# Filler matmuls ahead of the first back, transposes in the fronts' PSUM banks, other ranks in the planner: a retention layer with a mixer

## The chip, the cores and the metric

The kernel runs on one core of one Trainium2 chip. The metric is the device time of one launch in microseconds (us), from the first to the last instruction and what lies around them. The engines are PE (matmuls), DVE and ACT and POOL (elementwise work), and SP, which here issues DMAs. Each works through its own queue in the order of the program; they meet at semaphores.

## What is computed

A recurrent retention layer over 768 positions with 8 heads, and behind it an MLP mixer over positions and channels:

```python
B, H, S, D = q.shape                      # 4, 8, 768, 64
gamma = 1.0 - 2.0 ** (-5.0 - np.arange(H, dtype=np.float32))
scale = 1.0 / np.sqrt(D)
for t in range(S):
    state = gamma[None, :, None, None] * state + np.einsum('bhd,bhe->bhde', k[:, :, t], v[:, :, t])
    y[:, :, t] = scale * np.einsum('bhd,bhde->bhe', q[:, :, t], state)
x = np.ascontiguousarray(y.transpose(0, 2, 1, 3)).reshape(B, S, H * D)
# mixer: w_tok1 768x256, w_tok2 256x768, w_ch1 512x1536, w_ch2 1536x512
xt = x.transpose(0, 2, 1)
h = np.maximum(xt @ w_tok1, 0.0) @ w_tok2
u = x + h.transpose(0, 2, 1)
h2 = np.maximum(u @ w_ch1, 0.0) @ w_ch2
return (u + h2).astype(np.float32)
```

## The kernel before

The recurrence is cut into six chunks of 128 positions. A *front* works on one batch b in four pairs p of heads, a *back* does the channel mixing of one batch. A pair goes through these steps, with the lines of the kernel before: three loads of k, q and v (SP, L209 and L213); a cast of k with the heads' decay on DVE (L230) and casts of q and v on POOL (L237); six transposes each of k and q on PE (L250) into a PSUM tile of the tag tp, and a copy from it to SBUF, on ACT for q, on DVE (first batch) or ACT for k (L259); ten small matmuls for the chunks' states (L272), which DVE chains in U (L281, L284) and ACT and DVE round to r (L291, L295); the scores in two halves of six matmuls (L311), masked by DVE (L318); the output y in two halves (L332, L335), scaled by ACT or DVE into x (L348, L352) and cast by POOL (L367). Then comes the token mixing of the pair's 128 channels: 12 matmuls with w_tok1 (L378), a ReLU on ACT (L384), two halves of six matmuls with w_tok2 (L396), additions to x on DVE (L403), casts to u on POOL (L410), transposes of u on PE (L420) into a tp tile and copies to uT on ACT (L429).

A back has two halves of 384 positions. A half has 48 matmuls with w_ch1 (L459), each group of four followed by a ReLU on ACT (L472), and then 36 with w_ch2 (L483), followed by additions on DVE (L491) and stores (L496). It needs uT of all four pairs, and it takes PSUM tiles of the tag ba.

PSUM has eight banks: one for tp, four for fa (scores, states, y, and the token mixing of batches 1 to 3), three for ba (backs, and the token mixing of the first front). A tile is taken by the first instruction that writes it, which waits until the last reader of the tile that had the bank is done.

The order of every engine's queue comes from a planner in the kernel, arrange. Each operation is an Op with an engine, a rank, an occupation and a latency in ns, what it depends on, and the tiles it takes and uses. The planner goes on with the operation that can start first; of those of one engine that can start within 20 ns of each other the lowest rank goes first. Fronts' ranks on PE begin with 0 and those of backs with 1, so front work goes ahead on PE and back work fills in; on the other engines it is the other way round. Within fronts the rank is (batch, pair, step):

```python
pr = (0, b, p, n[0]) if eng == "PE" else (1, b, p, n[0])
```

The numbers in the planner only set the order; on the chip the semaphores decide when an instruction starts. Loads of batch 1 wait for the weights up to the second third of w_ch2.

## Time and profile before

| | us |
|---|---|
| median of 3 runs | 228.26 (227.74 to 229.22) |
| the profiled execution | 229.68 |
| its span, first to last instruction | 228.0 |
| PE busy | 204.1, 90% |
| ACT busy | 115.9, 51% |
| DVE busy | 114.9, 50% |
| POOL busy | 68.6, 30% |

The rows below are from one profiled execution. Times are us from the start of its span. A row of a timeline gives the start, how long the group lasted, engine, line, operation, out<-in, shape, how many, and in brackets how long the engine sat idle before it and what ended that. In a row of stretches the engines stand in the order PE, PE's weight loads, DVE, ACT, POOL. Matmuls are pipelined, so the time of a short group holds the latency of its last one.

### The profile page before, as it was taken

How to read it: one execution, taken by the hardware profiler on the slowest of the kernel's cores; microseconds unless marked ns; L12 is line 12 of the kernel's file. 1: busy time of each engine (PE TensorE's matmuls, PEld its weight loads, DVE VectorE, ACT ScalarE, POOL GpSimd, SP SyncE). 2: the span in 40 equal slices, each digit the busy share in tenths (PEclk: the TensorE clock that was granted, in tenths of full speed). 3: DMA queues.
4: the chain of work that ended last, by engine and by line, in shares of the span. 5: the costliest groups of instructions: out<-in, count | busy, mean ns of one | idle time of the engine just before them, and what ended most of it. 6: DMA issues, size and time to landing. Idle time of an engine off the chain costs nothing.

```text
span 228.0 us, 4873 instructions
## 1 busy us (share of the span) xinstructions
PE 204.1 (90%) x1968; PEld 131.4 (58%) x1968; DVE 114.9 (50%) x287; ACT 115.9 (51%) x219; POOL 68.6 (30%) x120
## 2 busy tenths in 40 slices
PE   0467797799999999959999999999999999999993
PEld 0255596455576676746777757674554554645541
DVE  6388944101879888885799887621202103012021
ACT  2255346473599864557877741762360540721700
POOL 2429935831045347243355424130000000000000
PEclk9999999799999999988999999999999999999999
DMA  7999999999999999991000011101201202103012
GB/s 181 241 241 223 206 208 204 242 243 228 259 290 244 264 235 223 275 277 24 0 3 3 0 49 46 52 0 49 92 0 50 88 3 92 46 5 127 9 46 92
DMA packets 65814, 29.41 MB, mean 129 GB/s; under 512 B 50432, under 2 KB 62720, under 8 KB 65792
## 3 DMA queue, kind: packets, MB, share of 16 engines
q1 hardware_dynamic: 61568, 25.17, 47.6%
q0 software_dynamic: 4224, 3.93, 10.6%
q8 instruction: 15, 0.25, 0.5%
q14 instruction: 7, 0.06, 0.1%
HBM read 26.74 MB, written 6.29 MB: 145 GB/s over the span
## 4 chain that ended last, share of the span: by engine, by line
PE 77%; ACT 6%; DVE 5%; issue 3%; POOL 3%; SPq 3%; DMA 2%; DVEq 0%; POOLq 0%; ACTq 0%
PE ba L459 27%; PE ba L483 27%; PE tp L250 4%; PE fa L378 4%; ACT qT L259 4%; PE fa L311 3%; PE tp L420 3%; PE fa L396 3%; DMA vf<-in_v_dram 2%; PE fa L335 2%; DVE am L318 2%; PE ba L378 2%; PE fa L332 2%; SPq L213 1%; SPq L209 1%
## 5 line engine op out<-in xcount | busy, mean ns | idle before, releaser
L459 PE MATMUL ba<-uT,wc 128*128 128x384 f16 x384 | 71.8, 334 | 0.0
L472 ACT ACTIVATE h<-ba 128x384 f16<-128x384 f32 x96 | 47.0, 493 | 46.1 <-PE ba L459 45.7
L483 PE MATMUL ba<-wc,h 128*128 128x512 f16 x288 | 67.8, 379 | 0.0
L491 DVE TENSOR_TENSOR o<-x,ba 128x512 f32<-128x512 f32 x24 | 16.5, 686 | 74.7 <-PE ba L483 74.7
L459 PEld LDWEIGHTS <-wc 128*128 128x128 f16 x384 | 36.5, 100 | 23.1 <-issue 2.5
L483 PEld LDWEIGHTS <-h 128*128 128x128 f16 x288 | 26.5, 98 | 27.5
L318 DVE TENSOR_TENSOR am<-fa,mask 128x384 f16<-128x384 f32 x64 | 33.1, 549 | 9.4 <-PE fa L311 9.2
L259 ACT COPY qT<-tp 128x768 f16<-128x768 f16 x16 | 23.2, 1449 | 13.7 <-PE tp L250 13.1
L367 POOL CAST x<-x 128x384 f16<-128x384 f32 x32 | 16.6, 521 | 37.7 <-ACT x L348 34.4
L410 POOL CAST u<-x 128x384 f16<-128x384 f32 x32 | 15.9, 510 | 24.5 <-DVE x L403 24.2
L284 DVE SCALAR_TENSOR_TENSOR U<-U,gp,fa 128x64 f32<-128x64 f32 x64 | 17.5, 275 | 1.2
L348 ACT ACTIVATE x<-fa,gy 128x192 f32<-128x192 f32 x40 | 14.4, 420 | 6.7 <-PE fa L335 6.7
L230 DVE TENSOR_SCALAR k<-kf,gk 128x384 f16<-128x384 f32 x32 | 15.9, 537 | 3.4 <-DMA kf<-in_k_dram 3.3
L237 POOL CAST q<-qf 128x768 f16<-128x768 f32 x16 | 13.7, 858 | 12.0 <-DMA qf<-in_q_dram 8.3
L429 ACT COPY uT<-tp 128x768 f16<-128x768 f16 (+1 forms) x20 | 13.4, 672 | 7.6 <-PE tp L420 7.5
L403 DVE TENSOR_TENSOR x<-x,fa 128x384 f32<-128x384 f32 x24 | 12.5, 551 | 8.6 <-PE fa L396 7.4
L335 PE MATMUL fa<-v,am 128*128 128x64 f16 x192 | 15.9, 204 | 0.6 <-DVE am L318 0.6
L237 POOL CAST v<-vf 128x768 f16<-128x768 f32 x16 | 13.6, 851 | 8.8 <-PE fa L335 4.9
L335 PEld LDWEIGHTS <-am 128*128 128x128 f16 x192 | 13.9, 105 | 3.4 <-DVE am L318 1.0
L250 PE MATMUL tp<-ident,k 128*128 128x128 f16 x96 | 9.6, 248 | 6.8 <-DVE k L230 5.2
L378 PEld LDWEIGHTS <-wt 128*128 128x128 f16 x192 | 13.4, 107 | 3.0 <-issue 1.4
L311 PE MATMUL fa<-qT,kT 64*128 64x128 f16 x192 | 12.0, 237 | 2.8 <-ACT qT L259 2.7
(46 smaller groups left out, 184.2 us busy)
## 6 DMA issues: line engine op xcount, KB each, us to landing
kf<-in_k_dram SPq DMA_DIRECT2D x16, 384.0 KB, 6.5
qf<-in_q_dram SPq DMA_DIRECT2D x16, 384.0 KB, 6.0
vf<-in_v_dram SPq DMA_DIRECT2D x16, 384.0 KB, 5.7
out_dram<-o SPq DMA_DIRECT2D x24, 256.0 KB, 2.0
wc<-in_moe_w_ch_dram POOLq DMA_DIRECT2D x6, 512.0 KB, 9.9
wt<-in_moe_w_tok_dram POOLq DMA_DIRECT2D x2, 384.0 KB, 6.6
```

Source lines behind the costliest of these rows:

```text
L237: nc.gpsimd.tensor_copy(t.rearrange("p c h d -> p h c d"), src.tile.rearrange("p (h c) d -> p h c d", h=2))
L250: nc.tensor.transpose(tp[:, c * P:(c + 1) * P], src.tile[:, c].rearrange("p h d -> p (h d)"), ident16)
L259: (nc.scalar.copy if eng == "ACT" else nc.vector.tensor_copy)(d, o)
L284: nc.vector.scalar_tensor_tensor(U[:, c], U[:, c - 1], gp[:, p:p + 1], o, ALU.mult, ALU.add)
L311: nc.tensor.matmul(a[j][:, i], KT.tile[r, t], QT.tile[r, t], start=True, stop=True)
L318: nc.vector.tensor_tensor(am, src[:, :HC], mask, ALU.mult)
L335: nc.tensor.matmul(o[:, j * D:(j + 1) * D], AM[2 * hf + j].tile[:, i], V.tile[:, c, j], start=(c == 0), stop=(c == 0 or j == 1))
L367: nc.gpsimd.tensor_copy(X16.tile[:, half(hf)], X.tile[:, half(hf), pc])
L378: nc.tensor.matmul(acc[:, jt * P:(jt + 1) * P], wt1[:, i, jt * P:(jt + 1) * P], X16.tile[:, i], start=(i == 0), stop=(i == NC - 1))
L459: nc.tensor.matmul(acc[:, :SH], w[:, ct, (ft % FW) * P:(ft % FW + 1) * P], UT.tile[:, ct, sh * SH:(sh + 1) * SH], start=(ct == 0), stop=(c ...
L472: nc.scalar.activation(H2.tile[:, ft], A.tile[:, :SH], AF.Relu)
L483: nc.tensor.matmul(A.tile, H2.tile[:, ft, i * P:(i + 1) * P], wc2[ft // FW][:, ft % FW], start=(ft == 0), stop=(ft == NF - 1))
```

## The change

Four things are changed together. (1) When a PSUM tile is taken before the first back has begun, tile_of first puts matmuls of ident by ident into the tile's bank: as many as fit, at 60 ns each, into the gap that the planner saw on PE ahead of the operation. Their results are overwritten. (2) The tag tp is gone; transposes take banks of fa, or ba for u in the first front, and fa has five banks. (3) Ranks within a front go by step plus 1 (first batch) or 12 (others) times the pair, then by pair; the planner counts 1350 ns for the copy of qT on ACT in place of 700. (4) From batch 2 on, transposes of k and q and the state matmuls also wait for the last L390 (token mixing) of the batch before. Buffers of k16, q16, v16, kT, qT, U and r16 grow by one, h2 loses one.

```diff
--- before.py
+++ after.py
@@ -80,7 +80,7 @@
     )
     gyw = const_p.tile([P, H, D], FP, name="gyw")
     nc.vector.memset(gyw, 1.0)
-    NR = 3
+    NR = 4
     r16 = [const_p.tile([P, NC - 1, P], F16, name=f"r16_{i}") for i in range(NR)]
     for t in r16:
         nc.vector.memset(t, 0.0)
@@ -93,9 +93,10 @@
     wc2 = [const_p.tile([P, FW, C], F16, name=f"wc2_{i}") for i in range(NW)]
 
 
-    BUFS = dict(kf=4, qf=4, vf=4, k16=2, q16=2, v16=3, kT=3, qT=3, U=2, am=8, x16=2, h1=4, u16=3,
-                x=3, uT=3, h2=3, o=3, r16=NR, tp=1, fa=4, ba=3)
+    BUFS = dict(kf=4, qf=4, vf=4, k16=3, q16=3, v16=4, kT=4, qT=4, U=3, am=8, x16=2, h1=4, u16=3,
+                x=3, uT=3, h2=2, o=3, r16=NR, fa=5, ba=3)
     SEM, GUARD = 80, 100
+    EARLY, LATE = 1, 12
     ops = []
 
     class Slot:
@@ -159,9 +160,16 @@
             order.append(op)
         return order
 
+    idle = [0]
+
     def tile_of(slot, pool, shape, dtype, tag=None):
         tag = tag or slot.tag
         slot.tile = pool.tile(shape, dtype, name=tag, bufs=BUFS[tag])
+        if pool is ps:
+
+            for _ in range(idle[0]):
+                nc.tensor.matmul(slot.tile[:, :P], ident16, ident16, start=True, stop=True)
+            idle[0] = 0
         return slot.tile
 
 
@@ -170,11 +178,11 @@
     def weight(key, ns, out, src, dep):
         def emit():
             return nc.gpsimd.dma_start(out=out, in_=src.rearrange("(i p) j -> p i j", p=P))
-        wops[key] = Op("POOL", (0,) if key in ("t1", "t2", ("c1", 0)) else (1, 0, NP), 800, 800, emit, deps=[dep], dma=ns)
+        wops[key] = Op("POOL", (0,) if key in ("t1", "t2", ("c1", 0)) else (1, 0, 99), 800, 800, emit, deps=[dep], dma=ns)
 
 
     load_done = [None]
-    x_add, uT_done, y_done, t2_done = {}, {}, {}, {}
+    x_add, uT_done, y_done, t1_done, t2_done = {}, {}, {}, {}, {}
     xs, uTs = {}, {}
     rcount = [0]
 
@@ -185,7 +193,7 @@
 
         def op(eng, occ, lat, emit, deps=(), takes=(), uses=()):
             n[0] += 1
-            pr = (0, b, p, n[0]) if eng == "PE" else (1, b, p, n[0])
+            pr = (0 if eng == "PE" else 1, b, n[0] + (EARLY if first else LATE) * p, p)
             return Op(eng, pr, occ, lat, emit, deps, takes, uses, guard=g if eng == "PE" else 0)
 
         if p == 0:
@@ -227,9 +235,13 @@
             k16 = tile_of(K, sb, [P, NC, 2, D], F16)
             for j in range(2):
                 h = 2 * p + j
-                nc.vector.tensor_scalar(k16[:, :, j, :], sl["k"].tile[:, j * NC:(j + 1) * NC, :],
-                                        gk[:, h:h + 1], None, ALU.mult)
-        kc = op("DVE", 900, 980, emit, [ld["k"]], [K], [sl["k"]])
+                src = sl["k"].tile[:, j * NC:(j + 1) * NC, :]
+                if KENG == "ACT":
+                    nc.scalar.mul(k16[:, :, j, :], src, gk[:, h:h + 1])
+                else:
+                    nc.vector.tensor_scalar(k16[:, :, j, :], src, gk[:, h:h + 1], None, ALU.mult)
+        KENG = "DVE"
+        kc = op(KENG, 900, 980, emit, [ld["k"]], [K], [sl["k"]])
 
         def cast(slot, src):
             def emit():
@@ -242,14 +254,14 @@
         KT, QT = Slot("kT"), Slot("qT")
 
         def turn(src, dst, dep, eng):
-            T = Slot("tp")
+            T = Slot("fa")
 
             def emit():
-                tp = tile_of(T, ps, [P, 1024], F16)
+                T.tile = tp = tile_of(T, ps, [P, 512], FP).bitcast(F16)
                 for c in range(NC):
                     nc.tensor.transpose(tp[:, c * P:(c + 1) * P],
                                         src.tile[:, c].rearrange("p h d -> p (h d)"), ident16)
-            t = op("PE", 340, 500, emit, [dep], [T], [src])
+            t = op("PE", 340, 500, emit, [dep, t1_done.get(b * NP - 1) if b > 1 else None], [T], [src])
 
             def emit():
                 d, o = tile_of(dst, sb, [P, S], F16), T.tile[:, :S]
@@ -257,8 +269,8 @@
                     d = d.rearrange("d (f p i) -> d f i p", f=2, i=HC)
                     o = o.rearrange("d (f i p) -> d f i p", f=2, i=HC)
                 (nc.scalar.copy if eng == "ACT" else nc.vector.tensor_copy)(d, o)
-            return op(eng, 700 if eng == "ACT" else 470, 800 if eng == "ACT" else 560, emit,
-                      [t], [dst], [T])
+            occ = dict(ACT=1350 if dst is QT else 700, DVE=470)[eng]
+            return op(eng, occ, occ + 90, emit, [t], [dst], [T])
         kt = turn(K, KT, kc, "DVE" if first else "ACT")
         qt = turn(Q, QT, qc, "ACT")
 
@@ -271,7 +283,7 @@
                 for j in range(2):
                     nc.tensor.matmul(st[j * D:(j + 1) * D, c * D:(c + 1) * D], K.tile[:, c, j],
                                      V.tile[:, c, j], start=True, stop=True)
-        pp = op("PE", 300, 470, emit, [kc, vc, y_done.get(b * NP + p - 2)], [ST], [K, V])
+        pp = op("PE", 300, 470, emit, [kc, vc, y_done.get(b * NP + p - 2), t1_done.get(b * NP - 1) if b > 1 else None], [ST], [K, V])
         prev = None
         for c in range(NC - 1):
             def emit(c=c):
@@ -379,12 +391,14 @@
                                      X16.tile[:, i], start=(i == 0), stop=(i == NC - 1))
         t1 = op("PE", 690, 860, emit, x_ops + [wops["t1"], None if first else t2_done.get(b * NP + p - 1)], [T1], [X16])
 
+        t1_done[b * NP + p] = t1
+
         def emit():
             h1 = tile_of(H1, sb, [P, NJ, P], F16)
             nc.scalar.activation(h1.rearrange("p j c -> p (j c)"), T1.tile[:, :NJ * P], AF.Relu)
         hr = op("ACT", 300, 380, emit, [t1], [H1], [T1])
         tt = []
-        T = Slot("tp")
+        T = Slot(FA)
         for hf in range(2):
             T2, U16 = Slot(FA), Slot("u16")
 
@@ -410,11 +424,11 @@
                 nc.gpsimd.tensor_copy(u, X.tile[:, half(hf), pc])
             uc = op("POOL", 450, 510, emit, [ad], [U16], [X])
             if first:
-                T = Slot("tp")
+                T = Slot(FA)
 
             def emit(hf=hf, U16=U16, T=T):
                 if hf == 0 or first:
-                    tile_of(T, ps, [P, 1024], F16)
+                    T.tile = tile_of(T, ps, [P, 512], FP).bitcast(F16)
                 for i in range(HC):
                     c = hf * HC + i
                     nc.tensor.transpose(T.tile[:, c * P:(c + 1) * P], U16.tile[:, i], ident16)
@@ -519,7 +533,13 @@
             front(b, p)
     for b in range(B):
         back(b)
+    end, mixing = 2000, False
     for o in arrange():
+        if o.eng == "PE":
+            mixing = mixing or o.prio[0] == 1
+            if o.takes and not mixing:
+                idle[0] = max(0, int((o.start - end - 60) / 60))
+            end = o.start + o.occ
         o.ins = o.emit()
```

The first instructions of PE, the kernel before (tp takes the transposes of the first pair's k and q):

```order
L250 LDWEIGHTS k_141
L250 MATMUL tp<-ident_84,k_141 128x128
...
L250 LDWEIGHTS q_151
L250 MATMUL tp<-ident_84,q_151 128x128
...
L311 LDWEIGHTS kT
L311 MATMUL fa<-qT,kT 128x128
...
L272 LDWEIGHTS k_141
L272 MATMUL fa<-v_164,k_141 64x64
```

And of the changed kernel, where L171 is a filler, L262 a transpose, L284 a state matmul and L323 a score:

```order
L171 LDWEIGHTS ident_84
L171 MATMUL fa<-ident_84 128x128
...
L262 LDWEIGHTS k_143
L262 MATMUL fa<-ident_84,k_143 128x128
...
L284 LDWEIGHTS k_143
L284 MATMUL fa<-v_239,k_143 64x64
...
L323 LDWEIGHTS kT
L323 MATMUL fa<-qT,kT 128x128
...
L171 LDWEIGHTS ident_84
L171 MATMUL fa<-ident_84 128x128
L171 LDWEIGHTS ident_84
```

63 fillers stand ahead of the first transpose, 10 ahead of the transposes of q, 22 ahead of the states, and 61 behind the 12 scores, ahead of the transposes of the second pair. Over the whole first front there are 278.

The first front's token mixing on PE, before: 24 matmuls of L378 (two pairs), the output of the third pair, 18 of L396, and only then the second half of the fourth pair's scores (L311):

```order
L272 LDWEIGHTS k_350
...
L335 LDWEIGHTS am
...
L396 LDWEIGHTS wt_110
L396 MATMUL ba<-h_494,wt_110 128x128
L396 LDWEIGHTS wt_110
```

Changed, the same place (L390 is the token mixing's first product, L410 its second, L347 the output):

```order
L390 LDWEIGHTS wt_111
L390 MATMUL ba<-x_455,wt_111 128x128
L390 LDWEIGHTS wt_111
...
L323 LDWEIGHTS kT
L323 MATMUL fa<-qT,kT 128x128
L323 LDWEIGHTS kT
...
L323 LDWEIGHTS kT
...
L410 LDWEIGHTS wt_112
```

Both halves of the fourth pair's scores now stand between the 24 first products and the 18 second ones, and the second half of the third pair's output between the two.

The end of back 0 on PE, before, where L483 is its last matmuls, L420 the transposes of the last u of front 1, and L459 the first of back 1:

```order
L483 MATMUL ba<-wc_2_116,h_982 128x512
L332 LDWEIGHTS qT
L332 MATMUL fa<-r_2_105,qT 128x128
...
L420 MATMUL tp<-ident_84,u_1715 128x128
...
L420 MATMUL tp<-ident_84,u_1719 128x128
L311 LDWEIGHTS kT
L311 MATMUL fa<-qT,kT 128x128
...
L459 LDWEIGHTS wc_0_111
L459 MATMUL ba<-uT,wc_0_111 128x384
```

Changed, where L497, L434 and L473 stand for these:

```order
L497 MATMUL ba<-wc_2_118,h_1215 128x512
L434 LDWEIGHTS u_1883
L434 MATMUL fa<-ident_84,u_1883 128x128
...
L434 MATMUL fa<-ident_84,u_1892 128x128
L323 LDWEIGHTS kT
L323 MATMUL fa<-qT,kT 128x128
...
L497 MATMUL ba<-wc_2_118,h_1215 128x512
...
L473 LDWEIGHTS wc_0_113
L473 MATMUL ba<-uT,wc_0_113 128x384
```

The last transposes of u stood behind the last matmuls of back 0; now they stand ahead of the last two.

## Rows read from the trace of the kernel before

**Rows 1.** Stretches: us, busy us of each engine (instructions), clock, DMA share, GB/s
```profile
42.00:51.60 9.60, 9.60 (x52) 5.35 (x49) 0.84 (x2) 5.88 (x12) 4.73 (x9) 0.82 1.21 246
51.60:154.30 102.70, 98.35 (x1225) 68.45 (x1224) 76.92 (x187) 66.59 (x120) 41.01 (x69) 0.98 0.60 137
```

**Rows 2.** Chain of waits that ended last: start, us, what ran
```profile
42.12 9.48 PE ba L459 x48
...
54.62 0.34 PE tp L250 x6
...
66.45 0.67 PE fa L378 x12
...
154.26 7.77 PE ba L483 x36
162.03 7.80 PE ba L459 x48
...
216.54 7.78 PE ba L483 x36
224.34 0.69 DVE o L491
```

**Rows 3.** PE's waits in 0:42: us in total, times, longest
```profile
PE fa L311 <- ACT qT L259: 2.7, 2, 1.5
...
PE tp L420 <- ACT uT L429: 1.7, 3, 0.6
PE tp L250 <- ACT qT L259: 1.5, 1, 1.5
```

**Rows 4.** PE's waits in 45:155
```profile
PE tp L420 <- ACT qT L259: 2.7, 5, 1.5
PE fa L272 <- DVE U L284: 1.3, 1, 1.3
```

**Rows 5.** Timeline of PE, first front
```profile
26.76 0.50 PE L311 MATMUL fa<-qT,kT 64*128 64x128 f16 x6 [1.17 <-ACT qT L259]
27.19 2.74 PE L378 MATMUL ba<-x,wt 128*128 128x128 f16 x24
...
32.69 0.34 PE L311 MATMUL fa<-qT,kT 64*128 64x128 f16 x6
...
37.30 0.66 PE L378 MATMUL ba<-x,wt 128*128 128x128 f16 x9 [0.41 <-POOL x L367]
...
41.79 0.33 PE L420 MATMUL tp<-ident,u 128*128 128x128 f16 x3 [0.57 <-ACT uT L429]
```

**Rows 6.** Stretches around the two falls of the clock, columns as in rows 1
```profile
40.00:42.00 2.00, 0.86 (x10) 0.66 (x10) 0.06 (x1) 0.96 (x2) 1.95 (x6) 1.00 1.06 222
42.00:44.00 2.00, 2.00 (x12) 1.04 (x9) 0.69 (x2) 0.97 (x2) 2.00 (x6) 0.64 1.01 257
44.00:46.00 2.00, 2.00 (x8) 0.98 (x7) 0.15 (x1) 0.98 (x2) 1.07 (x2) 0.50 1.34 243
96.00:98.00 2.00, 0.70 (x18) 0.58 (x16) 1.86 (x7) 0.03 (x1) 2.00 (x4) 1.00 1.18 269
98.00:100.00 2.00, 0.52 (x14) 0.50 (x14) 1.97 (x5) 1.77 (x2) 1.32 (x3) 1.00 1.04 219
100.00:102.00 2.00, 2.00 (x27) 1.79 (x25) 1.48 (x5) 0.81 (x2) 0.40 (x1) 0.65 1.03 327
102.00:104.00 2.00, 2.00 (x12) 1.16 (x11) 1.25 (x5) 1.26 (x3) 0.00 (x0) 0.50 0.65 144
```

**Rows 7.** Timeline of POOL: ident is made
```profile
1.24 0.29 POOL masks.py:199 TENSOR_SCALAR_AFFINE_SELECT ident<-ident 128x128 f16<-128x128 f16 x1
```

**Rows 8.** Page, part 5: costliest groups, busy us, mean ns, idle before
```profile
L410 POOL CAST u<-x 128x384 f16<-128x384 f32 x32 | 15.9, 510 | 24.5 <-DVE x L403 24.2
...
L403 DVE TENSOR_TENSOR x<-x,fa 128x384 f32<-128x384 f32 x24 | 12.5, 551 | 8.6 <-PE fa L396 7.4
```

**Rows 9.** Timeline of SP: first load of batch 1
```profile
39.30 0.37 SPq L213 DMA_DIRECT2D kf<-in_k_dram  x1
```

## Prediction

> **What bounds the kernel now.** I read the end of the chain of waits first. From 154.26 us PE runs second-stage matmuls of the channel mixing (L483) and first-stage ones (L459) with no wait, until an addition on DVE at 224.34 ends the compute [rows 2]. Each half of a back has 36 L483 in 7.77 and 48 L459 in 7.80, 15.57 us, and a launch has eight halves, 124.6 us of PE. These cannot begin before the first front has ended: the first 48 L459 start at 42.12 [rows 2]. Between the two PE interleaves front work with backs; in 51.6:154.3 it is busy 98.35 of 102.70 us [rows 1]. So after 42.12 the kernel is bound by PE, and the end moves with three things only: when PE gets its first L459, how long PE waits between 42 and 154, and how long it runs at the lower clock in there.
>
> Start: until 42 us PE waits for others. Copies of qT and uT on ACT, which hold the single bank of the tag tp, are behind 2.7, 1.7 and 1.5 us of it [rows 3]. In this time PE is also slow. 24 matmuls of 128 columns take 2.74 us at 27.19 [rows 5], less the latency of the last about 0.111 us each; later 12 of them take 0.67 [rows 2], 0.056 each. These are the two levels, 1.2 and 2.4 GHz (the granted clock reads 1.00 up to 42, since no change is recorded yet; the durations tell the level). PE had run without a wait from 26.76 to 32.69 before the durations halved, 5.9 us [rows 5].
>
> Middle: the waits of 4.3 us are nearly all on qT copies (2.7) and the state chain U (1.3) [rows 4], and they lie together: PE is busy 0.70 of 2 us in 96:98 and 0.52 in 98:100 [rows 6]. There back 0 has run out of matmuls and front 1 is not done.
>
> Clock: after the thin stretch 40:42 (0.86 busy) the granted clock is 0.64 and 0.50 in 42:46, after 96:100 it is 0.65 and 0.50 in 100:104 [rows 6]. (0.36+0.50)x2 = 1.7 us of full-speed work is lost the first time and (0.35+0.50)x2 = 1.7 the second. The first shows in L459: 48 take 9.48 instead of 7.80 [rows 2].
>
> **The change, part by part.** *Fillers.* 278 matmuls of 128 columns are added, all before the first L473 (the old L459). None costs anything where PE would wait for data, 0.056 us each where it would not; a filler goes into the bank of the operation behind it, so it also waits until that bank is free, and it stands ahead of everything in PE's queue. I therefore take the first front of the changed kernel as a queue and count it. Before the first L390 (token mixing, the old L378) stand 241 fillers and 166 other matmuls: 407 x 0.056 = 22.8 us. They can start when ident is made, at 1.24+0.29, so 1.6 with the signal [rows 7]. The first 63 run without a gap, so by the rise in [rows 5] the first 5.9 us, 53 of them, are at the lower level: 53 x 0.055 = 2.9 us more. First L390: 1.6+22.8+2.9 = 27.3 us, against 27.19 before [rows 5]: the fillers eat what the ranks and banks free here. Bounds: 24.4 if no filler is slow; 30.0 if the 2.7 us of waits on qT [rows 3] come on top.
>
> *Order and warm clock after that.* Before, PE goes from 27.19 to the last nine L378 of the front at 37.30 [rows 5], 10.1 us: 5.5 of it at the lower level, and pair 3's second half of L311 waits for a bank until 32.69. Now both halves of pair 3 stand ahead of the token mixing's second product, and between the first L390 and the last twelve stand 122 matmuls, fillers among them: 6.9 us at 0.056; with 0.3 for the last masks on DVE, 7.1 or so. Last L390: 34.4.
>
> *Tail.* Before, from 37.30 to the first L459 at 42.12: 4.8 us. Now L390 0.67, then 18 L410 (the old L396), 9 transposes and 8 fillers, 2.0; an addition on DVE 0.55 (L403) and signals 0.1; ten fillers 0.56, which stand behind the bank that this addition frees and so run after it; two groups of transposes with four fillers, 0.56; the last copy 0.3: 4.7. The transposes no longer wait for one bank, but the fillers take that back. The cast on POOL, 0.51 [rows 8], hides under the ten fillers; without them it would stand there itself. First L473 at 39.1: **-3.0 us**. With 24.4 and 30.0 in place of 27.3 it is 36.2 or 41.8, so -5.9 to -0.3.
>
> *Clock at the first L473.* 20 fillers and the rest keep PE at some 2.3 busy us in the last 3 before it, where 40:42 had 0.86 of 2. I take the fall as gone: **-1.7** [rows 2], bound 0.
>
> *Banks, ranks, and the hand-over at the end of back 0.* The 2.7 us on qT [rows 4] are u's transposes waiting for tp while ACT empties qT from it; the 1.3 us are L272 waiting for U. Now the transposes draw on five banks, U has three buffers, and the planner counts the qT copy at 1350 ns, not 700. By the third order above, the last transposes of u stand ahead of the last two L497, and behind them 28 more front matmuls cover the copy to uT. Ahead of them, between the second token product and the transposes, PE has ten L284, six L497 and six L262, some 1.9 us, against two additions of 0.55 and a cast of 0.51 [rows 8], 1.7 with signals, if nothing of front 2 stands ahead of them on DVE. One cast of k does. I keep 1.6 us of waits from 4.3: **-2.7**; bounds 0 and -4.3. With short waits the second fall of the clock goes too: **-1.7**, bound 0.
>
> *Serial fronts, other buffers.* That front b waits for the last L390 of front b-1 adds no work; it costs PE only if the back runs out, which is the hand-over above. h2 with two buffers suffices, as halves of a back follow each other. Loads: those of batch 1 start at 39.30, when the weights are in [rows 9], and the first transposes of front 1 come at 54.62 [rows 2]; in the new order at 39.1+7.8+5.2 = 52.1, still 12.8 us behind the issue. What covers them is back 0 itself; a load that came later than that would stop PE by as much.
>
> Sum: -3.0-1.7-2.7-1.7 = -9.1. The profiled execution took 229.68 (span 228.0), so 220.6; the median is 228.26, so **219.2**.
>
> **Rivals.** *The hand-over still breaks* (front 1 is as late as before, PE waits 4 us, the clock falls): only the first two terms hold, 228.3-4.7 = 223.6. For it: DVE is busy 1.86 and 1.97 of 2 us there [rows 6], and none of its work goes away. Against: both tiles that were waited for get more room.
>
> *The first front is not shorter* (the fillers run behind late data): the -3.0 falls, 222.2. For it: a group of 61 stands ahead of pair 1's transposes. Against: the count has little room for waits. Both together: 226.6.
>
> *The clock falls again at the first L473*, 1.7 us, 220.9. For it would be short waits at many places in the tail, one per bank. The trace speaks against it: the level fell only after 40:42. The Trainium skill (TensorE: Matmul & The Clock Gate, "A second HAM failure mode: psum-queue depth-cycling") says that PE pausing briefly between groups as it cycles banks is enough to make the clock swing; this front cycles five banks. By that rule the time would be this rival's.
>
> *Slower: the fillers run at the lower level.* If PE never rises before 39 us, each of the other 529 matmuls of the first front (582 less 53) costs 0.055 more, 29 us: 228.3+29-6.1 = 251. The gain is used up at 9.1/0.055 = 165 more slow matmuls, 9 us. For it: between 14 and 27 us before, PE worked with gaps and did not rise. Against: 63 in one run are longer than the stretch in which it rose.
>
> *No change*: if ident's fillers neither lift the clock nor delay, and the new ranks do nothing, 228.
>
> **The numbers.** Forecast 0.49 (its own range 216 to 222), hand-over 0.19, late front 0.13, both 0.06, clock again 0.05, slow fillers 0.06, no change 0.02. Low end: start at 36.2 and no waits, -5.9-1.7-4.3-1.7 = -13.6, 214.7; the ends of both bounds seldom meet, so I stop at 215.5. High end: beyond the hand-over rival with a start one us late, 225. Some 1% is what a measurement of this kernel tells from no change. Faster by over 1% (under 226.0): all but the last two, "both" and a little, 0.85; within 1% 0.09; slower 0.06.
>
> **What would show it.** First L390 near 27 us, first L473 near 39, its 48 in 7.8; granted clock 1.00 from about 8 us on, up to the pure back; PE's waits between 52 and 150 under 2 us, none over 1; the pure back from about 147 to 215. Wrong would be: a first L473 after 41, a wait of over 1 us ahead of batch 1's first L473, or 128-column fillers at 0.11 us after 10 us.

## The result

The changed kernel takes 221.79 us (median of 4, 218.98 to 222.94) beside 228.74 (227.74 to 229.28) for the kernel before, a ratio of 0.9625 [0.9521, 0.9729]; sampled again it takes 221.27 (median of 6, 218.52 to 225.48), ratio 0.9577 [0.9531, 0.9624]. The forecast of 219.2 (215.5 to 225.0) holds both medians and is 2.1 to 2.6 us below them. Five of its ten executions took over 1.5% more than the fastest of their sample, the first profiled one (222.45 us) among them, and the ratios leave these out. The rows below come from the profiled execution of the second sample (219.29 us, span 217.6) unless the text says otherwise.

The chain of waits that ended last (start, us, what ran), to be read beside [rows 2]. Line numbers have moved: L459 is now L473, L483 L497, L378 L390, L396 L410, L420 L434, L250 L262, L272 L284, L491 L505.

```profile
40.11 7.80 PE ba L473 x48
...
159.45 7.77 PE ba L497 x36
...
213.97 0.69 DVE o L505
```

The first 48 L473 start 2.01 us earlier than in [rows 2] and take 7.80 instead of 9.48. From their start to the last addition pass 173.86 us; before it was 182.22.

Stretches (columns as in [rows 1]): from the first L473 on, then those that answer to the second thin place of [rows 6].

```profile
40.00:50.00 10.00, 10.00 (x62) 5.72 (x59) 0.00 (x0) 6.52 (x14) 3.79 (x9) 1.00 1.11 213
50.00:155.00 105.00, 104.82 (x1269) 71.15 (x1268) 81.73 (x192) 67.49 (x124) 41.23 (x71) 1.00 0.67 153
...
96.00:98.00 2.00, 2.00 (x37) 1.74 (x35) 0.99 (x4) 1.63 (x5) 0.00 (x0) 1.00 1.23 281
98.00:100.00 2.00, 2.00 (x27) 1.25 (x25) 2.00 (x5) 1.94 (x4) 1.00 (x2) 1.00 1.20 279
```

PE stands still for 0.18 us in 50:155 and the granted clock is 1.00 throughout; before, 4.35 us of idle time lay in 51.6:154.3 [rows 1], and 96:100 was the thin place [rows 6]. The view of PE's waits in 45:155, which before gave [rows 4], is empty now.

PE's waits in 0:42 (us in total, times, longest), beside [rows 3]; L171 is the line of the fillers.

```profile
PE fa L171 <- POOL ident masks.py:199: 1.6, 1, 1.6
PE ba L171 <- DVE x L417: 0.6, 2, 0.4
PE fa L171 <- DVE am L330: 0.5, 1, 0.5
PE fa L284 <- POOL v L249: 0.5, 1, 0.5
```

Timeline of PE at the points that the forecast named, beside [rows 5]:

```profile
27.59 1.68 PE L390 MATMUL ba<-x,wt 128*128 128x128 f16 x24
...
34.73 0.83 PE L390 MATMUL ba<-x,wt 128*128 128x128 f16 x12
...
38.84 0.72 PE L171 MATMUL ba<-ident 128*128 128x128 f16 x10 [0.38 <-DVE x L417]
...
39.95 5.36 PE L473 MATMUL ba<-uT,wc 128*128 128x384 f16 x32
```

The first and the last L390 are where the queue count put them (27.3 and 34.4); the tail is half a microsecond longer. PE's stretch up to the first L390:

```profile
0.00:27.60 27.60, 24.41 (x408) 22.96 (x409) 18.36 (x66) 11.10 (x18) 12.90 (x24) 1.00 1.07 208
```

In the first profiled execution, the fourth pair's v came so late that its cast waited 3.62 us and PE 2.7 behind it, PE did nothing in 26:28, the granted clock fell behind that (0.59 in 28:30, 0.56 in 30:32), and the first L473 started at 43.25. The rows are POOL's timeline and PE's waits of that execution:

```profile
27.67 0.82 POOL L249 CAST v<-vf 128x768 f16<-128x768 f32 x1 [3.62 <-DMA vf<-in_v_dram]
```
```profile
PE fa L284 <- POOL v L249: 2.7, 1, 2.7
```

### The profile page after: what moved, and what is told of

Read it like the earlier page. It is cut to its first block, busy times and chain, and to the rows that moved or that the text cites. A ratio compares the mean times of both kernels' runs of the same rounds, so it can differ in the third digit from the quotient of the medians.

```text
span 220.7 us, 5421 instructions
## 1 busy us (share of the span) xinstructions
PE 210.4 (95%) x2246; PEld 141.4 (64%) x2246; DVE 117.1 (53%) x288; ACT 114.4 (52%) x219; POOL 67.4 (31%) x120
## 3 DMA queue, kind: packets, MB, share of 16 engines
q0 software_dynamic: 4224, 3.93, 11.3%
## 4 chain that ended last, share of the span: by engine, by line
PE 83%; SPq 7%; DMA 5%; DVE 3%; issue 1%; POOL 0%; DVEq 0%
PE ba L473 29%; PE ba L497 28%; DMA vf<-in_v_dram 5%; SPq L217 4%; PE fa L410 4%; PE fa L390 4%; SPq L221 3%; PE fa L262 3%; PE fa L323 3%; PE fa L347 2%; PE fa L344 2%; PE fa L434 2%; PE fa L284 2%; PE ba L390 2%; DVE x L417 1%; PE ba L410 1%
## 5 line engine op out<-in xcount | busy, mean ns | idle before, releaser
L497 PE MATMUL ba<-wc,h 128*128 128x512 f16 x288 | 68.7, 379 | 0.0
L473 PE MATMUL ba<-uT,wc 128*128 128x384 f16 x384 | 68.4, 326 | 0.0
L505 DVE TENSOR_TENSOR o<-x,ba 128x512 f32<-128x512 f32 x24 | 16.5, 686 | 66.5 <-PE ba L497 66.4
L473 PEld LDWEIGHTS <-wc 128*128 128x128 f16 x384 | 35.8, 98 | 22.0
L497 PEld LDWEIGHTS <-h 128*128 128x128 f16 x288 | 26.1, 98 | 26.7
L330 DVE TENSOR_TENSOR am<-fa,mask 128x384 f16<-128x384 f32 x64 | 33.6, 552 | 10.6 <-PE fa L323 10.4
L379 POOL CAST x<-x 128x384 f16<-128x384 f32 x32 | 16.0, 508 | 38.4 <-ACT x L360 24.3
L271 ACT COPY qT<-fa 128x768 f16<-128x768 f16 x16 | 23.3, 1453 | 8.5 <-PE fa L262 8.5
L171 PE MATMUL fa<-ident 128*128 128x128 f16 x251 | 18.5, 231 | 2.5 <-POOL ident masks.py:199 1.6
L171 PEld LDWEIGHTS <-ident 128*128 128x128 f16 x278 | 18.2, 104 | 4.2 <-POOL ident masks.py:199 1.6
L242 DVE TENSOR_SCALAR k<-kf,gk 128x384 f16<-128x384 f32 x32 | 17.5, 589 | 1.5 <-DMA kf<-in_k_dram 1.4
L443 ACT COPY uT<-fa 128x768 f16<-128x768 f16 x12 | 9.6, 801 | 11.3 <-PE fa L434 11.3
L347 PE MATMUL fa<-v,am 128*128 128x64 f16 x192 | 14.2, 195 | 0.0
L390 PEld LDWEIGHTS <-wt 128*128 128x128 f16 x192 | 12.5, 102 | 2.1
L347 PEld LDWEIGHTS <-am 128*128 128x128 f16 x192 | 12.5, 99 | 1.5 <-DVE am L330 0.2
```

Source lines behind the costliest of these rows:

```text
L171: nc.tensor.matmul(slot.tile[:, :P], ident16, ident16, start=True, stop=True)
L242: nc.vector.tensor_scalar(k16[:, :, j, :], src, gk[:, h:h + 1], None, ALU.mult)
L271: (nc.scalar.copy if eng == "ACT" else nc.vector.tensor_copy)(d, o)
L330: nc.vector.tensor_tensor(am, src[:, :HC], mask, ALU.mult)
L347: nc.tensor.matmul(o[:, j * D:(j + 1) * D], AM[2 * hf + j].tile[:, i], V.tile[:, c, j], start=(c == 0), stop=(c == 0 or j == 1))
L390: nc.tensor.matmul(acc[:, jt * P:(jt + 1) * P], wt1[:, i, jt * P:(jt + 1) * P], X16.tile[:, i], start=(i == 0), stop=(i == NC - 1))
```

## The experiments

Times are medians; "first back" is the start of the first 48 back matmuls in the chain, "rest" the time from there to the last addition on DVE, "idle" PE's idle time in 45:155, all of the profiled execution.

| kernel | us | range | ratio to before | first back | rest | idle |
|---|---|---|---|---|---|---|
| before | 228.74 | 227.74-229.28 | | 42.12 | 182.22 | 4.35 |
| changed (a_again) | 221.27 | 218.52-225.48 | 0.9577 [0.9531, 0.9624] | 40.11 | 173.86 | 0.18 |
| changed, no fillers (a_nofill) | 217.79 | 217.52-218.69 | 0.9517 [0.9479, 0.9554] | 38.73 | 173.90 | 0.18 |
| before + fillers (b_fill) | 231.30 | 230.26-231.59 | 1.0100 [1.0066, 1.0134] | 44.84 | 180.45 | 4.34 |
| before + qT number (b_qt) | 221.46 | 221.13-221.92 | 0.9672 [0.9635, 0.9708] | 41.27 | 175.07 | 1.00 |
| changed, wide fillers (a_fill512) | 218.55 | 218.10-218.73 | 0.9562 [0.9508, 0.9617] | 39.25 | 173.86 | 0.18 |
| changed, first 63 fillers (a_f63) | 218.67 | 217.68-221.21 | 0.9556 [0.9488, 0.9624] | 39.26 | 173.90 | 0.18 |
| wide fillers in 12 to 25 only (w_fill) | 218.52 | 218.00-218.82 | 0.9546 [0.9516, 0.9576] | 39.65 | 173.86 | 0.18 |
| no fillers, old banks (n_tp) | 222.57 | 221.19-224.35 | 0.9747 [0.9657, 0.9837] | 39.63 | 177.59 | 3.26 |
| no fillers, old ranks (n_rank) | 222.84 | 221.57-224.10 | 0.9753 [0.9684, 0.9821] | 39.65 | 177.97 | 2.46 |
| no fillers, no serial rule (n_noser) | 221.80 | 221.38-222.23 | 0.9691 [0.9662, 0.9721] | 39.56 | 177.33 | 2.47 |
| no fillers, old qT number (n_qt700) | 221.13 | 220.76-222.34 | 0.9670 [0.9623, 0.9717] | 40.48 | 175.61 | 1.60 |
| no fillers, weights later (w_wt) | 219.37 | 218.92-219.49 | 0.9582 [0.9554, 0.9610] | 37.97 | 175.62 | 1.89 |

**The kernel as it is, once more (a_again).** Nothing is edited.

> The changed kernel once more, unaltered. In its profiled execution the first L473 began at 43.1 us, because v of the fourth pair landed at 27.6 and PE stood 2.7 us for it, and the clock fell; two of its four runs were 3 us shorter. Theory 1 (the late load is a race of the loads with the weights, which goes either way): times spread over 218 to 223 us, and a profile with a short time shows no wait of PE above 1 us before 39 us, a clock of 1.00 up to the first L473, and that first L473 at about 39.5. Theory 2 (the fillers alone set the start, whatever the loads do): the first L473 is at 42 to 43 us in every profile, and short runs gain elsewhere.

Measured: 221.27, with executions from 218.5 to 225.5. Its ten executions of both samples lie between 218.5 and 225.5, the fourteen of the kernel before beside it between 227.2 and 229.8. The profile is as theory 1 had it for a short time: after the start PE waits 0.6 us at most, and the first L473 comes at 39.95. The spread goes beyond the 223 that it gave. The late v of the first profile is seen in a weaker form here too (cast of the fourth v at 25.80 after a wait of 1.82 us; 23.57 before).

**No fillers (a_nofill).** All 278 fillers are left out and nothing else.

```diff
-                idle[0] = max(0, int((o.start - end - 60) / 60))
+                idle[0] = 0
```

> The changed kernel without its 278 fillers, order otherwise the same. Theory 1 (fillers give the warm clock and cost little): PE is at the lower level up to about 30 us, the clock falls near the first L473 as before (48 L473 in about 9.4 us), the stretch after is as in the changed kernel: 2 to 4 us slower than it, about 223 to 225 us. Theory 3 (fillers hold PE up more than the clock gives): the first L473 comes 2 us earlier than with them, and the time is 219 or less. The middle (no waits of PE between 50 and 150 us) should be the same in both theories.

Measured: 217.79, the fastest kernel of this study, and by its ratio 0.6 points under the changed kernel. The two intervals overlap a little, so the times alone do not settle it. The two profiles differ by 1.38 us at the first back and by 0.04 after it. Chain, stretches and PE's timeline:

```profile
38.73 7.80 PE ba L473 x48
...
212.63 0.69 DVE o L505
```
```profile
20.00:24.00 4.00, 1.76 (x18) 1.24 (x19) 3.51 (x12) 1.10 (x1) 2.85 (x5) 0.62 1.35 209
24.00:28.00 4.00, 3.61 (x49) 3.26 (x49) 2.60 (x8) 2.07 (x7) 2.58 (x4) 0.52 1.18 187
```
```profile
11.59 0.82 PE L262 MATMUL fa<-ident,q 128*128 128x128 f16 x6
...
33.94 0.83 PE L390 MATMUL ba<-x,wt 128*128 128x128 f16 x12
...
38.56 7.96 PE L473 MATMUL ba<-uT,wc 128*128 128x384 f16 x48
```

Here PE does what the fillers are there to prevent. Six transposes take 0.82 us up to 12 us (0.51 at the upper level), and from 21 to 28 us the granted clock is at the lower level again. Still the first L473 starts 1.38 us earlier than with the fillers, and its 48 take 7.80: the clock does not fall there. Of the 1.38 us, 0.79 are there at the last L390 (33.94 against 34.73) and 0.60 come in the tail (4.62 against 5.22). So the warm first front is real, and here the fillers cost more than it gives, as theory 3 expected.

**Fillers alone (b_fill).** The kernel before with the fillers and nothing else of the change (the same loop in `tile_of`, the same rule for their number, which gives 314 here).

> The kernel before with fillers only, put in by the same rule; banks, ranks and planner as before. Theory 1: the first front runs warm, the first 48 L459 take 7.8 instead of 9.5 us, the first L459 is 1 to 3 us earlier, and the wait and the fall of the clock at 96 to 104 us stay: 224 to 226 us. Theory 3 (fillers hold PE up): first L459 at 42 us or later, 227 to 229 us.

Measured: 231.30, slower than before by 1.0% [0.7, 1.3] and slower than either theory had it. PE's waits, in 0:45 and in 45:155:

```profile
PE tp L169 <- ACT uT L435: 1.7, 3, 0.6
...
PE tp L426 <- ACT qT L265: 2.7, 5, 1.5
PE fa L278 <- DVE U L290: 1.3, 1, 1.3
```

The waits for uT stand ahead of the fillers now (L169) with the same 1.7 us, and the fillers run after them, ahead of the real transposes. The first back matmuls start at 44.84 in place of 42.12; they take 7.80, so the fall of the clock is gone, 1.68 us gained for 2.72 lost. The waits of [rows 4] are unchanged: fillers do not reach the hand-over.

**One number of the planner alone (b_qt).** The kernel before; only the copy of qT on ACT is planned to occupy ACT for 1350 ns and not 700 (and to be done after 1440 and not 800; the 800 of ACT's other copies becomes 790).

```diff
-            return op(eng, 700 if eng == "ACT" else 470, 800 if eng == "ACT" else 560, emit,
-                      [t], [dst], [T])
+            occ = dict(ACT=1350 if dst is QT else 700, DVE=470)[eng]
+            return op(eng, occ, occ + 90, emit, [t], [dst], [T])
```

> The kernel before with one number of the planner changed: 1350 ns for the copy of qT on ACT, as in the change; tp keeps its one bank. Theory A (the 4.3 us of waits in the middle came from a planner that took the copy at half its time): the waits between 45 and 155 us fall under 1.5 us and the second fall of the clock goes: 223 to 225 us. Theory B (they came from the single bank of tp and the two buffers of U): waits of 3 us or more stay, 227 to 229 us.

Measured: 221.46. One number gives 7.6 of the 11.3 us that lie between the kernel before (229.09 in these rounds) and the fastest one, with the old banks, buffers and ranks, and more than theory A's 223 to 225. Chain and PE's waits in 45:155:

```profile
41.27 7.80 PE ba L459 x48
...
216.34 0.69 DVE o L491
```
```profile
PE tp L420 <- ACT kT L259: 0.7, 1, 0.7
PE fa L335 <- DVE am L318: 0.3, 1, 0.3
```

The 2.7 us on qT and the 1.3 on U of [rows 4] are gone; PE idles 1.00 us in 45:155 where it idled 4.35, and both falls of the clock are gone with them, the first although PE is busy only 0.83 of 2 us in 38:40 and 1.40 in 40:42. How long that copy takes stood on the page of the kernel before (costliest groups: instructions, then busy us, mean ns of one):

```profile
L259 ACT COPY qT<-tp 128x768 f16<-128x768 f16 x16 | 23.2, 1449 | 13.7 <-PE tp L250 13.1 <-PE fa L335 0.6
```

It takes 1449 ns; with 800 in the plan, the transposes of u stand in PE's queue behind a bank that the plan frees 0.65 us too early.

**How wide the fillers are (a_fill512), how early (a_f63), and where (w_fill).** a_fill512 issues a quarter as many fillers, four times as wide (72 of them); a_f63 keeps only the first 63, which stand ahead of the first transposes; w_fill keeps wide ones only in the gaps that the planner sees between 12 and 25 us of its time.

```diff
-            for _ in range(idle[0]):
-                nc.tensor.matmul(slot.tile[:, :P], ident16, ident16, start=True, stop=True)
+            for _ in range((idle[0] + 2) // 4):
+                nc.tensor.matmul(slot.tile[:, :4 * P].rearrange("p (r c) -> p r c", r=4), ident16,
+                                 ident16.rearrange("p (r c) -> p r c", r=1).broadcast_to([P, 4, P]), start=True, stop=True)
```

> The changed kernel with its fillers four times as wide: each of the 278 fillers of 128 columns becomes a quarter as many of 512 columns, for the same PE time in the same places. Theory 'instructions' (the loads of 12 to 24 us run slower because PE's many extra instructions have to be fetched): the loads keep 230 GB/s and more between 12 and 24 us, the fourth v is cast by 24, the first L473 is at about 38.9, median 217.5 to 218.8. Theory 'activity' (they run slower because PE works and reads and writes there): rates below 200 GB/s in 12 to 24 remain, first L473 after 40, median 220.5 to 222. Theory 'hold' (fillers stand in front of real matmuls): loads at 230 GB/s and more, yet the first L473 after 40, median 219.5 to 221.

> The changed kernel with only the first run of 63 fillers (from 1.6 to 6.6 us), none of the other 215. Theory 'instructions' or 'activity': those between 10 and 25 us did the harm, so the loads of 12 to 24 us keep 230 GB/s and more and the median is 217.3 to 218.3, the same as without any filler. If the first 63 do the harm as well (loads before 12 us late): 219 to 221. If a warm clock from 8 us is worth something: the clock does not fall between 20 and 28 us and the first L473 comes before 38, median 216 to 217.

> The changed kernel with wide fillers (512 columns) only in the gaps that the planner sees between its times 12 and 25 us, 37 of them, none at the start and none near the end of the first front. Theory 'hold' (late fillers stand ahead of real matmuls and cost 0.4 us at the end; a full clock between 20 and 28 us is worth about 1 us): clock 1.00 to the end of the first front, first L473 at 37.6 to 38.4, median 216.6 to 217.6. Rival 'the clock of the first front does not matter, since its loads and copies bound it': first L473 at 38.6 to 39.2, median 217.5 to 218.6.

Measured: 218.55, 218.67 and 218.52, three times the same, each with the first back 0.5 to 0.9 us later than without fillers. Stretches of a_fill512, w_fill and a_f63:

```profile
24.00:28.00 4.00, 3.60 (x63) 2.76 (x61) 3.37 (x10) 2.44 (x7) 2.85 (x6) 1.00 1.12 155
```
```profile
24.00:28.00 4.00, 3.60 (x51) 2.01 (x49) 3.41 (x10) 2.49 (x4) 2.71 (x5) 1.00 1.00 147
```
```profile
12.00:28.00 16.00, 11.52 (x143) 9.41 (x142) 13.57 (x37) 8.76 (x17) 10.77 (x16) 0.52 1.18 213
```

a_fill512 and w_fill keep the granted clock at 1.00, a_f63 loses it from 12 to 28 us (0.52), and their times end alike. What w_fill was to gain (a first back at 37.6 to 38.4, 216.6 to 217.6 us) did not come. Its rival, that loads and copies bound the first front and not PE's clock, has the median right, but the first back at 39.65 is outside its 38.6 to 39.2 too. Of the loads, a_fill512 moved 242, 266, 219 and 268 GB/s in the 2 us stretches from 12 to 20 us (a_nofill 242, 259, 224 and 283) and had the fourth v cast at 23.20 (23.15 there). Median and cast are what its theory "instructions" expected; its sign in the rates, 230 GB/s and more up to 24 us, tells nothing, since a_nofill does not reach it either (211 and 207 in 20:24). "Activity" expected a first back after 40 and did not get it, though PE is as busy with wide fillers as with narrow ones (3.62 and 3.62 of 4 us in 20:24). In time alone the two are not apart: the ratios of wide and narrow fillers overlap, and the spread of 0.6 us in place of 7 is that of four executions. a_f63 lies between what it had for harmless fillers (up to 218.3) and for harmful ones (from 219).

The 0.5 to 0.9 us left are lost in different places. a_fill512 has its last L390 at 33.74, 0.20 earlier than a_nofill, and then needs 5.35 for the tail in place of 4.62: there fillers follow a wait and run ahead of the transposes behind it, as at 38.84 above. This is the "hold" of the expectations. a_f63 and w_fill have no filler in the tail and need the same 4.62 as a_nofill. They are late ahead of it: in a_f63 the first 24 L390 take 2.75, at a lower clock for longer than in a_nofill (2.12), and in w_fill they take 1.50 but start at 28.04 (26.51 there). So the clock of that stretch does show in PE's time, and no placing of fillers tried here gained by it; why w_fill's L390 start late was not taken apart.

**Undoing one other part at a time (n_tp, n_rank, n_noser, n_qt700).** All four are without fillers, so they are compared with a_nofill (217.79). n_tp gives the transposes their own bank again (`tp=1, fa=4`, and Slot("tp") at three places); n_rank sets the ranks back to pair, then stage (and the rank of the later weights' transfers, which is not shown below, with them); n_noser drops the dependences on t1_done; n_qt700 plans the qT copy at 700. No run takes back the added buffers alone, so what they are worth is not shown.

```diff
-                x=3, uT=3, h2=2, o=3, r16=NR, fa=5, ba=3)
+                x=3, uT=3, h2=2, o=3, r16=NR, tp=1, fa=4, ba=3)
```
```diff
-            pr = (0 if eng == "PE" else 1, b, n[0] + (EARLY if first else LATE) * p, p)
+            pr = (0, b, p, n[0]) if eng == "PE" else (1, b, p, n[0])
```
```diff
-            t = op("PE", 340, 500, emit, [dep, t1_done.get(b * NP - 1) if b > 1 else None], [T], [src])
+            t = op("PE", 340, 500, emit, [dep], [T], [src])
```
```diff
-            occ = dict(ACT=1350 if dst is QT else 700, DVE=470)[eng]
+            occ = dict(ACT=700, DVE=470)[eng]
```

> The changed kernel without fillers, and with the banks as before (one bank for transposes alone, four for the fronts). Theory 'the planner's number does it' (the qT copy planned at 1350 and the fillers are all that matters; the bank pool is a side matter): 217 to 219.5 with no wait over 1 us between 45 and 150. Rival 'the banks are part of the gain': qT or kT copies are waited for by the transposes between 45 and 150 again, 0.5 to 2 us in sum, and the first front is longer by up to 2 us, median 219.5 to 222.

> The changed kernel without fillers, and with the ranks by pair and then stage as before. Theory 'the ranks shorten the first front': first L473 at about 41 (41.27 in the kernel before with only the qT number changed) instead of 38.73, median 220 to 221.5; no wait over 0.7 us between 45 and 150. Rival 'the five shared banks shorten it': first L473 stays at 38.5 to 39.5, median 217.5 to 218.5.

> The changed kernel without fillers, and without the rule that a later front may take no bank before the front ahead of it has issued its first mixing matmuls (the dependences on t1_done of the transposes and of the state product). Theory 'the rule is needed': waits for qT, U or x of 0.5 to 3 us in sum come back between 45 and 150, median 218.5 to 221. Rival 'the rule is moot beside the qT number and the shared banks': no wait over 0.5 us there, median 217.3 to 218.5. The first front is the same in both (first L473 at 38.5 to 39.2), since the rule touches only the third and fourth batch.

> The changed kernel without fillers, and with the planner's qT copy back at 700. Theory 'the number does it, whatever the banks': copies planned 0.65 us too short leave PE waiting for qT between 45 and 150 again, over 1 us in sum with one of 0.7 or more, first L473 up to 1 us later, median 219.5 to 222. Rival 'five shared banks and the ranks make the number moot': no wait over 0.5 us there, median 217.3 to 218.5.

Measured: 222.57, 222.84, 221.80 and 221.13. Each is 3.3 to 5.1 us slower than a_nofill, so taking any one of the four out of this kernel costs time, and the rivals that called a part moot are out. PE's waits in 45:155 of n_tp, n_rank, n_noser and n_qt700:

```profile
PE tp L434 <- ACT qT L271: 1.6, 1, 1.6
PE fa L410 <- DVE am L330: 0.7, 1, 0.7
```
```profile
PE fa L284 <- DVE am L330: 0.8, 1, 0.8
PE fa L434 <- POOL u L424: 0.6, 1, 0.6
```
```profile
PE fa L262 <- DVE x L417: 1.0, 2, 0.8
PE fa L323 <- ACT qT L271: 0.8, 1, 0.8
```
```profile
PE fa L262 <- ACT qT L271: 0.5, 2, 0.3
```

The first back comes 0.8 to 1.75 us later in all four, most with the old number (40.48). It does so in n_noser too (39.56), where it was expected unchanged, since the rule touches the third and fourth batch only; that of n_rank (39.65) is nearer to the rival's 38.5 to 39.5 than to the theory's 41. The rest is in the middle: 1.4 to 3.1 us more idle time than the 0.18 of a_nofill. But what PE waits for is another thing each time (am, u, x, qT), in n_rank with a fall of the clock behind it (0.83 in 90:100). The waits expected by name came only in part: qT in n_tp with 1.6, x and qT in n_noser, in n_qt700 0.5 on qT in two places and little more elsewhere, where over 1 was expected; in n_rank, a wait of 0.8 where none over 0.7 was. n_tp, n_rank and n_noser are also slower than the slowest that was expected of them (222, 221.5 and 221). The parts do not add either: the number alone brings the kernel before 7.6 us, and taking it out of a_nofill costs 3.3.

**A control: another place for two transfers (w_wt).** a_nofill, with POOL issuing the token weights after the third v cast and not after the third q cast.

```diff
-    after = {"t1": casts[2][1], ("c1", 0): casts[3][1]}
+    after = {"t1": casts[2][2], ("c1", 0): casts[3][1]}
```

> The changed kernel without fillers, and with the two token weights' transfers issued by POOL after the third v cast instead of after the third q cast. Theory 'the 1.76 us of issuing them ahead of that cast delays PE': the third v cast comes at 16.7 to 17.5 instead of 18.42, PE's wait of 1.06 for it is gone, and the first L473 comes 0.5 to 1 us earlier, 217.0 median. Rival 'it comes back as a wait for the weights or for the casts behind five issues in a row': PE waits for the token weights or for x ahead of the first L390, first L473 at 38.7 to 40, median 217.8 to 219.5.

Measured: 219.37. Chain, and PE's waits in 45:155:

```profile
37.97 7.80 PE ba L473 x48
...
213.59 0.69 DVE o L505
```
```profile
PE fa L434 <- POOL u L424: 1.3, 2, 0.8
PE ba L473 <- ACT uT L443: 0.4, 1, 0.4
```

The start is as the theory said: the first back is 0.76 us earlier, although PE waits 0.5 us for the token weights and 0.3 for x, as the rival had it. The median lies in the rival's range, but for a reason that neither named: the planner's whole order moved, and 1.7 us of waits appeared at 83 to 90 us, 65 us behind the edit, at places that have nothing to do with the weights. This edit touches no bank, rank or number of the middle, and it costs there (rest 175.62 against 173.90) as much as the old qT number does (175.61). So the four runs above show that the order with all parts together is the good one; they do not show that each part's own mechanism is worth 3 to 5 us, since an edit without any such mechanism loses 1.7 in the same way. How much of each loss is mechanism and how much is a reshuffled order stays open. The same holds for the 7.6 us of b_qt: that the waits on qT went there speaks for the number, but no control was made in the old kernel.

## Why the prediction held, point by point

**First L473 at 39.1.** 39.95 came. The count of PE as a queue met the last L390 and the first (27.59 and 34.73 against 27.3 and 34.4), in part by luck: up to the first, PE was busy for 24.41 us where 25.7 were counted, and waited 1.6 us after its start where no wait was counted. The tail was sized at 4.7 and took 5.2; without fillers it is 4.6 (33.94 to 38.56). In the profiled execution the term is -2.0 and not -3.0; in the first profiled one it was +1.1 (43.25). What failed are two steps. One let a filler cost nothing wherever PE waits for data anyway, and had the cast on POOL hide under the ten fillers of the tail, so that the tail would be as long without them: it is 0.60 shorter. The other left the loads out: the fourth v was cast 2.7 and 4.5 us later than without fillers (25.80 and 27.67 against 23.15), PE waited 0.5 and 2.7 for it, and the bound of 30.0 for the first L390 was passed once (30.12). Of these 2.7 and 4.5, 1.5 and 1.1 are a later issue of that load (17.78 and 17.38 against 16.25), and 1.2 and 3.4 a longer time from issue to landing (8.0 and 10.2 against 6.8). The last section has what goes with the later issue; what made the landing longer is not shown. The prediction did say that the fillers "eat what the ranks and banks free here"; without them the first L390 starts at 26.51. It also put the 2.7 us on qT of [rows 3] down to the one bank of tp; that row is of scores (L311), which wait for the copied qT itself.

**Clock at the first L473, -1.7.** The size is right, 7.80 for 9.48. The reason, that the fillers keep PE busy ahead of it, is not needed: without any filler these 48 take 7.80 as well (a_nofill, b_qt), and with fillers in the old order too (b_fill). How busy PE is just ahead does not settle it either. In n_tp it was less busy there than in the kernel before (1.73 of 4 us; 1.13 and 0.86 in 38:42 before), and nothing fell; the rows are its 36:44:

```profile
36.00:40.00 4.00, 1.73 (x18) 1.12 (x16) 0.68 (x2) 2.24 (x5) 3.10 (x7) 1.00 1.22 203
40.00:44.00 4.00, 4.00 (x28) 2.47 (x27) 0.56 (x2) 3.24 (x8) 1.76 (x5) 1.00 1.08 252
```

**Hand-over, -2.7.** All of it went, 4.35 us of idle time down to 0.18, so the term was under-sized by 1.5. The prediction took the tiles that were waited for, gave them more room, and left 1.6 us for the chain of additions and casts between the second token product and the transposes. Two runs show that there were two ways. The planner's number alone takes 3.35 of the 4.35 (b_qt), and the banks, buffers, ranks and serial rule without the number and the fillers take 2.75 (n_qt700), as much as the term; only together is nearly all gone. The prediction named that number in half a sentence, did not hold it against the 1449 ns on the page, and priced it with nothing of its own.

**Second fall of the clock, -1.7.** The size is right: the thin stretch is gone and the clock stays at 1.00. That a thin stretch brings the fall is only in part borne out. In n_rank one comes back and the clock falls behind it; in n_tp, in the same place and thinner, it does not. Rows of n_rank and of n_tp:

```profile
88.00:92.00 4.00, 2.56 (x39) 1.92 (x37) 3.86 (x9) 3.89 (x5) 2.98 (x5) 1.00 1.22 238
92.00:96.00 4.00, 3.33 (x38) 2.62 (x38) 2.77 (x8) 2.29 (x6) 0.51 (x1) 0.67 1.19 298
```
```profile
88.00:92.00 4.00, 2.22 (x36) 1.77 (x35) 3.90 (x16) 2.84 (x4) 2.50 (x4) 1.00 1.12 254
92.00:96.00 4.00, 3.77 (x52) 2.86 (x52) 3.95 (x8) 3.79 (x8) 1.62 (x3) 1.00 1.19 287
```

So what PE must do to keep the level stays open, and that both falls went may hold some luck.

**Sum.** Forecast for the profiled execution 220.6, measured 219.29: -2.0, -1.7, -4.2 and -1.7 make -9.6, and the end moved by 10.4; where the 0.8 left lie was not traced. The sum comes within 1.3 us because errors cancel: the start fell short by 1.0, the hand-over gave 1.5 more, and the 0.8 came on top. The medians lie above that; the other profile of the changed kernel, 222.45, is the one with the late v, and what made its other executions differ is not known. **Range.** 221.8 lies inside; the spread of this kernel alone, 7 us, was not foreseen.

**Rivals.** "The hand-over still breaks" and "slow fillers" did not occur: 61 narrow fillers took 3.57 us. "The first front is not shorter" did, in the first profile, but by late loads and not by late data ahead of pair 1. "The clock falls again" did not: 48 in 7.80 or 7.81 in every kernel of the table but the one before (in n_tp in two pieces, 0.97 and 6.83). The Trainium skill (TensorE: Matmul & The Clock Gate, "A second HAM failure mode: psum-queue depth-cycling") would have short pauses between bank groups be enough for a swing; no run here shows that at this place, with five shared banks and pauses of 0.2 to 0.4 us in the tail. No rival said that the fillers are a loss and the rest of the change worth more without them, which is the best kernel here.

## What to carry to other kernels

Measure the durations that a planner uses before changing its rules: correcting one copy that was planned at half its time brought the kernel before 7.6 us here. In the changed order the same number is worth 3.3, so a part's price depends on what stands beside it. Do not count on a warm clock in a stretch that waits for loads and copies: no placing of fillers tried here paid. Look first whether the stretch ends earlier where the clock is up, and price the added instructions in the queue that they stand in and in the loads beside them. When an order is made by a greedy planner, test a part together with an unrelated edit of the same size of disturbance: here one such control moved the middle by 1.7 us, so a difference of that size says nothing on a part.

## What the hardware showed that was not expected

Transfers of instructions and longer issues of loads come together. The trace has a DMA queue of the kind "instruction", q8, which moves about 16 KB at a time. Of the 14 profiled executions of this study, nine have none of q8's between 8 and 18 us (before, b_qt, a_nofill, w_fill, w_wt and the four n_ kernels), and in all nine SP takes the same time for the last five loads' issues: 2.12 to 2.14, 0.51, 2.23 to 2.27, 2.00 to 2.02 and 0.54 to 0.55 us. The five others have one or two, and in all five the issue under way then, or the next one, is longer: the q at 9.25 takes 3.62 in the first profile of the changed kernel, the v at 11.66 takes 1.07 in b_fill, the last v 1.24 in a_fill512. Rows of SP's timeline, of a_again and of a_f63, with the instruction queue's row in 10:12 and in 12:14 (packets, MB, share of 16 engines):

```profile
11.59 1.91 SPq L221 DMA_DIRECT2D vf<-in_v_dram  x1
...
17.78 0.97 SPq L221 DMA_DIRECT2D vf<-in_v_dram  x1
```
```profile
q8 instruction: 1, 0.02, 4.0%
```
```profile
12.13 3.08 SPq L221 DMA_DIRECT2D kf<-in_k_dram  x1
...
17.26 0.52 SPq L221 DMA_DIRECT2D vf<-in_v_dram  x1
```
```profile
q8 instruction: 1, 0.02, 4.1%
```

More instructions ahead of the loads' end bring the next transfer forward into them: two in the kernel with 278 narrow fillers (10:12 and 16:18), one with 72 wide ones (14:16) or with the first 63 alone (12:14), none with 37 wide ones that start later. That they fall together in 14 of 14 is shown; that the transfer itself holds up SP's issue, and why by 0.4 to 1.5 us when its own share of the engines is 4% of 2 us, was not taken apart. A second queue of that kind, q14, moves about 9 KB at a time; the one of its transfers that meets one of these issues with no q8 transfer beside it (a_f63, within 14:16) meets one of 1.96 us, no longer than elsewhere. A longer issue alone does not make v late either: in b_fill, a_fill512 and a_f63 the cast of the fourth v does not wait for its load.
